# Half of the channel transform's outputs by plain float32 products, the rest by sums and differences

## The chip, the cores and the metric

The kernel runs on one core of a Trainium2 chip. The metric is the device time of one execution in microseconds (us). The core's engines are PE (matrix products; PEld is its weight load), DVE (VectorE), ACT (ScalarE), POOL (GpSimd) and SP, which here only issues DMAs. Each works through its own queue in order; they wait for each other through semaphores.

## The reference

The input is x of 2048 positions x 640 channels, float32. Two layers follow, each of a Fourier step and an attention step:

```python
def _A_ref(x, dft_seq_re, dft_seq_im, dft_hid_re, dft_hid_im):
    a = jnp.einsum("bsd,ed->bse", x, dft_hid_re)
    b = jnp.einsum("bsd,ed->bse", x, dft_hid_im)
    return jnp.einsum("ts,bse->bte", dft_seq_re, a) - jnp.einsum("ts,bse->bte", dft_seq_im, b)

def _B_ref(x, wqkv, wo):            # linear attention, 32 heads of 20
    q, k, v = ...                   # x @ wqkv
    phi = lambda t: jnp.where(t > 0, t + 1, jnp.exp(t)) + 1e-6
    kv = einsum(phi(k), v); z = sum(phi(k)); o = (phi(q) @ kv) / (phi(q) . z)
    return o @ wo

for _ in range(2):
    x = x + _A_ref(_layernorm(x), ...)
    x = x + _B_ref(_layernorm(x), B_wqkv, B_wo)
```

The matrices dft_hid_re and dft_hid_im are cosines and sines of 2 pi e d / 640. Cosine is even and sine odd under d -> 640 - d. Under e -> 320 - e both keep their size, and the sign depends on whether d is even or odd.

## The kernel before, in words

The 2048 positions are held as 16 tiles X[0] to X[15] of 128 x 640, in an order of positions and channels that puts mirror images side by side. The kernel trusts the symmetry of the four DFT matrices; `Check` compares all mirrored entries while the program runs, on DVE, and a slow general path stands behind a flag.

The Fourier step folds first: `script` walks a table of words (START for layer 0, SECOND for layer 1) and writes out, in that order, the sums and differences of mirrored channels (`f`, `d`), the layer norm, the sums and differences of mirrored positions, and the first part of the position transform (five sums of 512 columns, `u`). A word's last letter names the engine. Fetches of the channel matrices (`W`) and their split into a high and a low part (`w` on ACT, `v` on DVE) stand in the same tables. SECOND runs beside layer 0's attention outputs; each `|` is a pause until the next tile.

Then PLANS gives the order of the rest: `o1` is `outputs(1)`, the channel transform of one half of the positions; `s..` are the six other position sums (`whole`); `o0` is `outputs(0)`, the channel transform of the other half. In each `outputs` there are four groups r = 0 to 3. For each, `hidden` makes a real and an imaginary part in PSUM; ACT copies the imaginary part out, DVE forms difference and sum (`ym`, `yp`), and DVE and POOL add them to two tiles X (`lo` and `hi`), half a row at a time. `hidden` contracts over three blocks of 128 channels; each block takes three products of 322 columns in the split format (high x high, high x low, low x high), so nine a part. `keep` puts a position sum into SBUF as that high and low part: a copy on ACT and a subtraction on DVE.

The attention step follows at once. For each of the 16 tiles in turn (`keys_values`, tile positions n = 0 to 15) a tile is normalized, transposed on PE (L201) or through DMA, split, and multiplied with the key and the query weights (`product`, L250). Tile position n = 0 is X[8]; position 1 is X[11]. The layer norm's mean and variance come from DVE or ACT; the reciprocal root (`kept`, L163) and the shift (`nb`, L173) always come from POOL, in whose queue they stand behind the additions of `outputs`. `pksum`, the sum of the keys, is added up partly on POOL (L425).

Outside `script` a scheduler orders each engine's queue; it goes by a simulated timeline and the offsets of the AHEAD table, and the order is fixed when the program is built.

## Time and profile before

| | |
|---|---|
| median of 3 runs | 744.34 us (743.99 to 746.61) |
| span of the profiled execution | 742.7 us |
| PE busy | 722.4 us, 97% of the span |
| DVE, ACT, POOL busy | 599.4, 384.4, 262.9 us |
| granted PE clock | 0.997 over the span |
| DMA | 105.10 MB, mean 142 GB/s |

The span is the time from the first to the last instruction of one profiled execution; that execution's device time outside the profiler is not recorded, and the median of the runs lies 1.6 us above the span. In the rows of the timeline the first number is the start in us from the span's beginning, the second how long the engine was in it, then engine, line, operation, tiles and shapes, and the count; in brackets stands the idle time ahead and what ended it. PE's records overlap their successors, so a rate is read from start to start.

### The profile page before, as it was taken

Reading aid. Unit: us, or ns where it says so; the run is one execution under the profiler, and the core shown is the slowest. Engines: PE = TensorE matmul, PEld = TensorE weight load, DVE = VectorE, ACT = ScalarE, POOL = GpSimd, SP = SyncE. Lnnn points to the kernel's source line nnn. Section 1 sums busy time; section 2 is a strip of 40 time slices with the busy share of each in tenths; the row PEclk is TensorE's granted clock in tenths of the full one; section 3 lists DMA queues with packets and bytes.
Section 4 is the critical chain, followed back from the end, with each engine's and each line's share of the span. In section 5 each row is a group of like instructions: output and inputs, shape, how many; then the busy total and the mean of one; then the engine's idle time right before and its main releaser. Section 6 shows DMA issues by size and latency. Waiting matters only on the chain.

```text
span 742.7 us, 12890 instructions
## 1 busy us (share of the span) xinstructions
PE 722.4 (97%) x4762; PEld 691.3 (93%) x4762; DVE 599.4 (81%) x1147; ACT 384.4 (52%) x723; POOL 262.9 (35%) x293
## 2 busy tenths in 40 slices
PE   4899999999999999999999999999999999999997
PEld 1389999999999999899986999999999999999997
DVE  7999888878779785888887776967787888689983
ACT  7745654665445644445675337566632554443320
POOL 5237941331024311567772672136000010153220
PEclk9999999999999999999999999999999999999999
DMA  9333458562776836420001362645156663202553
GB/s 334 101 90 95 125 167 250 171 204 68 241 223 197 262 112 202 145 102 1 10 10 54 123 255 83 214 148 168 37 154 187 197 199 118 61 12 70 179 178 111
DMA packets 59005, 105.10 MB, mean 142 GB/s; under 512 B 5652, under 2 KB 23319, under 8 KB 58935
## 3 DMA queue, kind: packets, MB, share of 16 engines
q1 hardware_dynamic: 58935, 104.20, 44.2%
q8 instruction: 40, 0.66, 0.4%
q14 instruction: 30, 0.25, 0.1%
HBM read 78.99 MB, written 24.78 MB: 140 GB/s over the span
## 4 chain that ended last, share of the span: by engine, by line
PE 77%; DVE 11%; ACT 5%; DMA 2%; issue 1%; POOL 1%; SPq 1%; DVEq 0%; POOLq 0%; ACTq 0%
PE ps L250 49%; PE ps L355 16%; PE ps L1173 6%; PE ps L1099 4%; PE ps L201 2%; DVE w L189 1%; DVE t L189 1%; DMA raw<-in_wo 1%; DVE t L622 1%; DVE ps L615 1%; DVE ab L992 1%; DMA x<-in_x 1%; DVE x L644 1%; PE ps L543 1%; ACT ab L961 1%
## 5 line engine op out<-in xcount | busy, mean ns | idle before, releaser
L250 PE MATMUL ps<-w,t 128*128 128x320 f32 x2880 | 431.8, 310 | 0.5 <-DVE w L189 0.2
L250 PEld LDWEIGHTS ps<-w,t 128*128 128x128 f32 x2880 | 422.8, 188 | 1.4 <-DVE w L189 0.4
L355 PE MATMUL ps<-t,t 128*128 128x256 f32 (+1 forms) x640 | 139.8, 309 | 0.0
L1324 DVE CUSTOM_DVE_ANT_0 junk<-ck,ck 128x688 bf16<-128x688 f32 (+5 forms) x138 | 112.0, 812 | 8.2 <-DMA ck<-in_ck 6.6
L355 PEld LDWEIGHTS ps<-t,t 128*128 128x128 f32 x640 | 107.0, 188 | 0.0
L355 PE MATMUL ps<-w,t 128*128 128x384 f32 (+1 forms) x320 | 98.5, 310 | 0.6 <-DVE w L189 0.6
L388 ACT ACTIVATE t<-ps 128x640 f32<-128x640 f32 x64 | 45.1, 705 | 93.0 <-PE ps L250 89.3
L188 ACT CAST t<-t 128x640 fp32r<-128x640 f32 x62 | 45.1, 728 | 64.5 <-DVE t L218 29.3
L425 POOL TENSOR_TENSOR t<-t,s 128x640 f32<-128x640 f32 x17 | 30.5, 1792 | 118.0 <-DVE s L391 101.4
L599 POOL TENSOR_TENSOR t<-pq,t 128x640 f32<-128x640 f32 x25 | 40.0, 1610 | 74.6 <-ACT t L511 41.3
L355 PEld LDWEIGHTS ps<-w,t 128*128 128x128 f32 x320 | 60.1, 188 | 1.1 <-DVE w L189 0.9
L189 POOL TENSOR_TENSOR t<-t,t 128x640 fp32r<-128x640 f32 x14 | 22.8, 1631 | 92.8 <-ACT t L188 88.0
L189 DVE TENSOR_TENSOR t<-t,t 128x640 fp32r<-128x640 f32 x48 | 39.4, 820 | 15.6 <-ACT t L188 12.1
L391 DVE SCALAR_TENSOR_TENSOR pq<-t,pq 128x640 f32<-128x640 f32 x32 | 28.8, 899 | 23.8 <-ACT t L390 23.6
L390 ACT ACTIVATE t<-t 128x640 f32<-128x640 f32 x64 | 47.4, 741 | 0.0
L1173 PE MATMUL ps<-t,u 128*128 128x322 f32 x288 | 45.4, 314 | 0.4 <-DVE u L1156 0.4
L1173 PEld LDWEIGHTS ps<-t,u 128*128 128x128 f32 x288 | 43.2, 189 | 1.4 <-DVE u L1156 0.9
L188 ACT CAST t<-ps 128x640 fp32r<-128x640 f32 (+1 forms) x36 | 24.9, 691 | 35.5 <-PE ps L201 32.6
L391 DVE SCALAR_TENSOR_TENSOR s<-t,s 128x640 f32<-128x640 f32 x32 | 27.1, 847 | 15.8 <-ACT t L390 15.6
L1099 PE MATMUL ps<-cw,ab 128*128 128x512 f32 (+2 forms) x108 | 37.6, 500 | 2.0 <-ACT ab L962 1.2
L1099 PEld LDWEIGHTS ps<-cw,ab 128*128 128x128 f32 x108 | 19.9, 190 | 18.1 <-issue 12.9
L188 ACT CAST t<-s 128x640 fp32r<-128x640 f32 x32 | 23.3, 728 | 25.5 <-DVE t L189 18.6
(209 smaller groups left out, 1026.5 us busy)
## 6 DMA issues: line engine op xcount, KB each, us to landing
ck<-in_ck SPq DMA_DIRECT2D x48, 346.0 KB
ck<-in_ck SPq DMA_DIRECT2D x48, 344.0 KB
turn<-t SPq DMA_DIRECT2D x23, 320.0 KB
save<-w SPq DMA_DIRECT2D x20, 320.0 KB
w<-save SPq DMA_DIRECT2D x20, 320.0 KB
z<-turn SPq DMA_DIRECT2D x18, 320.0 KB
x<-in_x SPq DMA_DIRECT2D x16, 320.0 KB
out<-x SPq DMA_DIRECT2D x13, 320.0 KB
```

Source lines behind the costliest of these rows:

```text
L188: self.high = self.nc.scalar.copy(hi, src)
L189: return self.engine(pool).tensor_tensor(lo, src, hi.bitcast(F32), op=ALU.subtract)
L250: nc.tensor.matmul(pu[:m, 512 * h : 512 * h + HD], s, w[:, HD * h : HD * h + HD], start=first, stop=last)
L355: nc.tensor.matmul(self.place(G, c, part), x[:, 128 * c : 128 * c + 128], p[:, f : f + n], start=start and i == 0, stop=stop and i == 2, s ...
L388: nc.scalar.activation(h2(e), halves(pu), AF.Relu, scale=-1.0)
L390: nc.scalar.activation(e, e, AF.Exp, scale=-1.0)
L391: return k.ve.scalar_tensor_tensor(out, e, 1e-6, out, op0=ALU.add, op1=ALU.add)
L425: k.engine(n not in PKSUMS[k.layer]).tensor_tensor(pksum, pksum, pk, op=ALU.add)
L599: k.behind(k.nc.gpsimd.tensor_tensor(t1, self.PQ[self.order2[n]], self.zb, op=ALU.mult), lull)
L1099: self.k.nc.tensor.matmul(pu, s[:, cols : cols + 128], w[:, f : f + n], start=start and i == 0, stop=stop and i == len(todo) - 1)
L1173: self.k.nc.tensor.matmul(po[:, o : o + 322], s[:, f : f + 128], w[:, x, :], start=start, stop=stop)
L1324: i = nc.vector.tensor_tensor_reduce(k.junk[:, : a.shape[1]], b, a, 1.0, 0.0, op0, op1, o)
```

## The change

`hidden` now makes one plain float32 product for each of the three blocks, with 161, 322 and 161 columns, and with it only the outputs e = 0 to 160, for even and odd channels apart (the mirror e -> 320 - e then is a sum or a difference of the two). ACT and DVE form the real and imaginary parts' difference and sum as before, both into one tile `yy`; a new function `spread` adds the two parities for one set of outputs and subtracts them for the other, into `y`, with every second column written. One of its two instructions runs on DVE and one on POOL, in turns over the groups (SPREAD). The position sums are kept by one plain copy (`keep`), on ACT or DVE after KEPT and the tables, where there were a copy and a subtraction; the twelve memsets of `keep` on POOL go. The channel matrices are fetched whole (two DMAs of 128 x 644 a layer for six of 128 x 322) into work tiles, no longer through the `raw` buffers; their split goes, and one 2 x 161 scaling on ACT comes. The channels' order changes so that the two unmirrored channels stand first; the fold's slices and the layer norm's constants move with it. The check of the channel matrices compares eight or four mirror images in narrower pieces: 14 fetched tiles for 12, and one more checking step, at tile position 14 of layer 1.

The core of the diff:

```diff
-CKH = 344
-CKHN = 3
+CKH = (102, 135)
+CKHN = (2, 3)
+QN = 161
+HW = (0, 161, 483, 644)
+HP = (((0, 161), (0, 322), (161, 161)), ((161, 161), (0, 322), (0, 161)))
+SPREAD = ("vp", "pv")
-START = '... x11d f7v ... x01d k9a ... kda w02a fcv fdv w00a nfa w01a nea a3v b3v v00v c3v v01v t3v V1a v02v t1v t2v t0v w11a u23v w10a u21v u20v u24v v11v u22v w12a v12v v10v g0a ...'
+START = '... x11d W1d f7v ... x01d W0d w0a k9a ... kda fcv fdv nfa nea a3v b3v c3v t3v V1a t1v t2v t0v u23v u21v u20a u24a u22a g0a ...'
-SECOND = '... x11d W00d W01d W02d W10d | w00a | w01a v00W W11d | w02a v01v W12d | v02v | R0a V0a w10a | O0p sfa v10v ... | w11a c2v v11v H20v w12a nfa nea v12v ... u20v u21v u23v u24v u22v'
+SECOND = '... x11d W1d W0d w0a | | | | | R0a V0a | O0p sfa ... | c2v H20v nfa nea ... u20a u21v u23v u24a u22a'
+KEPT = ("ava", "vav")
...
-        steps = STEPS[0], STEPS[1] if ...
+        steps = STEPS[0] + (14,) * self.k.layer, STEPS[1] if ...
...
-    def hidden_fetch(self, par, c):
-        raw = self.k.raw.tile([128, 322], F32, tag="raw", name=self.k.nm("rawh"))
-        self.k.nc.sync.dma_start(raw, self.hid[par][c])
-    def hidden_high(self, par, c, raw): ...
-    def hidden_low(self, par, c, raw, eng): ...
+    def hidden_fetch(self, par):
+        t = self.k.temp(shape=(128, HW[3]))
+        self.k.nc.sync.dma_start(t, self.hid[par])
+        self.hw[par] = t
+    def hidden_scale(self):
+        self.k.nc.scalar.mul(self.hw[0][0:2, :QN], self.hw[0][0:2, :QN], 0.5)
...
     def keep(self, ci, c, pu, e=None):
-        hi, lo = (pool.tile([128, 640], F32R, tag=tag, name=k.nm("u")) for _ in range(2))
+        u = k.wp.tile([128, 640], F32, tag="w", name=k.nm("u"))
+        copy = nc.scalar.copy if e == "a" else nc.vector.tensor_copy
-            nc.scalar.copy(hi[:, :512], pu)
-            eng.tensor_tensor(lo[:, :512], pu, hi[:, :512].bitcast(F32), op=ALU.subtract)
+                copy(u[:, :512], pu)
...
     def hidden(self, ci, f, po, o):
-        order = (1, 2, 0) if ci == 3 else range(3)
+        order = (1, 2, 0) if ci == 3 else (1, 0, 2)
         for i, c in enumerate(order):
-            for s, x, start, stop in ((hi, 0, i == 0, False), (hi, 1, False, False), (lo, 0, False, i == 2)):
-                self.k.nc.tensor.matmul(po[:, o : o + 322], s[:, f : f + 128], w[:, x, :], start=start, stop=stop)
+            u, (at, n) = self.UT[min(ci, 2), c + 2 if ci == 3 else c], HP[ci % 2][c]
+            self.k.nc.tensor.matmul(
+                po[:, o + at : o + at + n], u[:, f : f + 128], self.hw[ci % 2][:, HW[c] : HW[c + 1]],
+                start=i == 0, stop=i == 2, skip_group_check=True,
+            )
+
+    def spread(self, y, x, by):
+        e = {"v": self.k.ve, "p": self.k.nc.gpsimd}
+        pairs = lambda t: t.rearrange("p g (b i) -> p g b i", b=2)
+        e[by[0]].tensor_tensor(y[:, :, 0 : 2 * QN - 1 : 2], x[:, :, :QN], x[:, :, QN:], op=ALU.add)
+        e[by[1]].tensor_tensor(
+            y[:, :, : 2 * QN - 2].rearrange("p g (b i two) -> p g b i two", b=2, two=2)[:, :, :, :, 1],
+            pairs(x[:, :, : QN + 1])[:, :, :, : QN // 2], pairs(x[:, :, QN - 1 :])[:, :, :, 1:], op=ALU.subtract,
+        )
...
-                nc.vector.tensor_tensor(ym, p[:, :322], yi, op=ALU.subtract)
-                nc.vector.tensor_tensor(yp, p[:, :322], yi, op=ALU.add)
+                nc.vector.tensor_tensor(yy[:, 0, :], p[:, :322], yi, op=ALU.subtract)
+                nc.vector.tensor_tensor(yy[:, 1, :], p[:, :322], yi, op=ALU.add)
+                self.spread(y, yy, SPREAD[r % 2])
```

How it moves the queues is shown at two places. In the changed program the lines of `product`, the transposes, the statistics and the key sum are L253, L204, L161/L166/L176 and L428 for L250, L201, L158/L163/L173 and L425; `hidden` is L1152 for L1173, and `spread` is L1161 (sums) and L1162 (differences).

The first place is layer 0, where `outputs(0)` begins and tile position 0 of the attention is transposed in its midst. POOL's queue before, from the last group of `outputs(1)` (L1216, L1205) to the reciprocal root of X[8] (kept_718):

```order
L1216 TENSOR_TENSOR x_130<-x_130,t_610 128x321
L1205 TENSOR_TENSOR x_124<-x_124,t_610 128x319
L1159 MEMSET u_642 128x31
L1159 MEMSET u_642 128x95
L158 TENSOR_SCALAR ve_719<-kept_718 128x1
L158 TENSOR_SCALAR ve_907<-kept_906 128x1
L1159 MEMSET u_656 128x31
L1159 MEMSET u_656 128x95
L158 TENSOR_SCALAR ve_1007<-kept_1006 128x1
L1159 MEMSET u_670 128x31
L1159 MEMSET u_670 128x95
L163 TENSOR_TENSOR kept_718<-ve_719,mhalf 128x1
```

and now (the root of X[8] is kept_620):

```order
L1161 TENSOR_TENSOR t_531<-t_530 128x322
L1210 TENSOR_TENSOR x_116<-x_116,t_512 128x321
L1211 TENSOR_TENSOR x_116<-x_116,t_512 128x319
L1198 TENSOR_TENSOR x_114<-x_114,t_512 128x319
L161 TENSOR_SCALAR ve_621<-kept_620 128x1
L161 TENSOR_SCALAR ve_766<-kept_765 128x1
L1210 TENSOR_TENSOR x_128<-x_128,t_531 128x321
L1211 TENSOR_TENSOR x_128<-x_128,t_531 128x319
L1198 TENSOR_TENSOR x_122<-x_122,t_531 128x319
L161 TENSOR_SCALAR ve_866<-kept_865 128x1
L166 TENSOR_TENSOR kept_620<-ve_621,mhalf 128x1
```

A `spread` instruction has joined each group, and the memsets are gone; the root still stands behind all four groups. PE's queue before (t_717 is X[8] normalized; t_386, t_392 and t_380 hold one channel matrix):

```order
L1173 MATMUL ps_767<-t_386,u_656 128x322 x2
L1173 MATMUL ps_767<-t_386,u_657 128x322
L1173 MATMUL ps_767<-t_392,u_670 128x322 x2
L1173 MATMUL ps_767<-t_392,u_671 128x322
L1173 MATMUL ps_767<-t_380,u_642 128x322 x2
L1173 MATMUL ps_767<-t_380,u_643 128x322
L201 MATMUL ps_786<-ident,t_717 128x128 x5
L1173 MATMUL ps_757<-t_426,u_683 128x322 x2
L1173 MATMUL ps_767<-t_426,u_683 128x322 x2
```

and now (t_619 is X[8] normalized; t_341 and t_238 hold the two channel matrices):

```order
L1152 MATMUL ps_659<-t_238,u_546 128x322
L1152 MATMUL ps_663<-t_238,u_546 128x322
L1152 MATMUL ps_659<-t_238,u_587 128x161
L1152 MATMUL ps_659<-t_238,u_553 128x161
L1152 MATMUL ps_663<-t_238,u_587 128x161
L1152 MATMUL ps_663<-t_238,u_553 128x161
L204 MATMUL ps_670<-ident,t_619 128x128 x5
L1203 MATMUL ps_690<-t_341,u_579 1x322
L1203 MATMUL ps_690<-t_341,u_570 1x161
```

The five transposes now follow both parts of two groups, where they followed the real parts alone.

The second place is layer 1, where `outputs(0)` ends and the attention begins. POOL's queue before, from the additions of the last groups to the key sum (kept_5087 and nb_5093 are the root and the shift of X[11], tile position 1; s_5085 are the keys of position 0):

```order
L1205 TENSOR_TENSOR x_100<-x_100,t_4998 128x319
L373 MEMSET t_5075 128x640
L1217 TENSOR_TENSOR x_110<-x_110,t_5026 128x319
L1205 TENSOR_TENSOR x_108<-x_108,t_5027 128x319
L162 TENSOR_SCALAR ve_5088<-kept_5087 128x1
L158 TENSOR_SCALAR ve_5183<-kept_5182 128x1
L163 TENSOR_TENSOR kept_5087<-ve_5088,mhalf 128x1
L163 TENSOR_TENSOR kept_5182<-ve_5183,mhalf 128x1
L173 TENSOR_TENSOR nb_5093<-kept_5087 128x1
L173 TENSOR_TENSOR nb_5190<-kept_5182 128x1
L175 TENSOR_SCALAR nb_5190<-nb_5190 128x1
L425 TENSOR_TENSOR t_5075<-t_5075,s_5085 128x640
```

and now (kept_4807, nb_4813 and s_4805):

```order
L1161 TENSOR_TENSOR t_4745<-t_4744 128x322
L376 MEMSET t_4795 128x640
L1211 TENSOR_TENSOR x_100<-x_100,t_4726 128x319
L1198 TENSOR_TENSOR x_98<-x_98,t_4726 128x319
L1198 TENSOR_TENSOR x_106<-x_106,t_4745 128x319
L165 TENSOR_SCALAR ve_4808<-kept_4807 128x1
L161 TENSOR_SCALAR ve_4903<-kept_4902 128x1
L1211 TENSOR_TENSOR x_108<-x_108,t_4745 128x319
L166 TENSOR_TENSOR kept_4807<-ve_4808,mhalf 128x1
L166 TENSOR_TENSOR kept_4902<-ve_4903,mhalf 128x1
L428 TENSOR_TENSOR t_4795<-t_4795,s_4805 128x640
L176 TENSOR_TENSOR nb_4813<-kept_4807 128x1
```

A `spread` instruction stands ahead of the last additions (one more a row before these), and the key sum has moved from behind the shift nb to ahead of it. PE's queue before, in the query product of tile position 0 (t_5086 is X[11] normalized; t_4923 and t_4924 are the split X[8]; t_5153 is the split X[11]):

```order
L250 MATMUL ps_5134<-w_5063,t_4924 128x320 x2
L250 MATMUL ps_5134<-w_5067,t_4923 128x320 x2
L201 MATMUL ps_5147<-ident,t_5086 128x128 x5
L250 MATMUL ps_5134<-w_5068,t_4923 128x320 x2
L250 MATMUL ps_5134<-w_5067,t_4924 128x320 x2
L250 MATMUL ps_5134<-w_5071,t_4923 128x320 x2
L250 MATMUL ps_5204<-w_5035,t_5153 128x320 x2
L250 MATMUL ps_5204<-w_5036,t_5153 128x320 x2
```

and now (t_4806 is X[11] normalized; t_4674, t_4675 and t_4873 are the split tiles):

```order
L253 MATMUL ps_4854<-w_4787,t_4675 128x320 x2
L253 MATMUL ps_4854<-w_4791,t_4674 128x320 x2
L253 MATMUL ps_4854<-w_4792,t_4674 128x320 x2
L253 MATMUL ps_4854<-w_4791,t_4675 128x320 x2
L204 MATMUL ps_4867<-ident,t_4806 128x128 x5
L253 MATMUL ps_4924<-w_4755,t_4873 128x320 x2
L253 MATMUL ps_4924<-w_4756,t_4873 128x320 x2
L253 MATMUL ps_4924<-w_4755,t_4874 128x320 x2
```

The transposes have moved from the midst of the query product to its end, and the next key product, which needs their split result, follows directly.

More of the change, by code (lines that the diff above doesn't have):

```diff
@@ L119, in __init__ @@
         nc.gpsimd.memset(self.tiny, 1e-6)
-        self.two = self.cst.tile([128, 2], F32, name="two")
-        nc.vector.tensor_scalar(self.two, self.ident[:, 0 : 65 : 64], -1.0, 2.0, op0=ALU.mult, op1=ALU.add)
     def nm(self, s):
@@ L803, in script @@
         order = [(w[0], int(w[1], 16), w[2:-1], w[-1]) for w in order.replace("|", "|0-").split()]
-        raw = {}
         summed = {i for kind, i, c, e in order if kind == "s" and e == "q"}
@@ L884, in script @@
             elif kind == "W":
-                raw[g, int(c)] = four.hidden_fetch(g, int(c))
+                four.hidden_fetch(i)
             elif kind == "x":
@@ L888, in script @@
             elif kind == "w":
[L889 to L893 removed]
+                four.hidden_scale()
             elif kind == "H":
@@ L899, in script @@
             elif kind == "u":
-                four.keep(2, int(c), four.sum(int(c)), eng)
+                four.keep(2, int(c), four.sum(int(c)), e)
             else:
@@ L1410, in fast_path @@
     pieces.sort(key=lambda p: p[0])
-    pieces += [(2 + m, 2 * m, ckh[m][f]) for m in range(2) for f in range(CKHN)]
+    pieces += [(2 + m, 4 if m or f > 1 else 0, ckh[m][f]) for m in range(2) for f in range(4 - m)]
     order = [0, 3, 4, 7, 1, 2, 5, 6]
```

134 lines of the change are left out of this document (65 added, 69 removed).

## The prediction, as it was written before the result was known

> **What bounds the kernel now.** I read the page first (busy shares and groups), then PE's timeline through the four stages that the change touches, then the queues of POOL, DVE and ACT at the places where PE goes on from a Fourier step into the attention.
>
> ```profile
> span 742.7 us, 12890 instructions
> PE 722.4 (97%) x4762; PEld 691.3 (93%) x4762; DVE 599.4 (81%) x1147; ACT 384.4 (52%) x723; POOL 262.9 (35%) x293
> L1173 PE MATMUL ps<-t,u 128*128 128x322 f32 x288 | 45.4, 314 | 0.4 <-DVE u L1156 0.4
> ```
>
> PE is busy 97% of the span; what shortens PE's own queue shortens the kernel, as long as no other engine's work then comes late. The channel products (L1173) are 288 records and 45.4 us, with 0.4 us of waiting. The stages on PE in layer 0 and in layer 1:
>
> ```profile
> 33.23 8.87 PE L1099 MATMUL ps<-cw,ab 128*128 128x512 f32 x20 [0.22 <-ACT ab L961]
> 41.65 11.38 PE L1173 MATMUL ps<-t,u 128*128 128x322 f32 x72
> 52.86 4.92 PE L1099 MATMUL ps<-cw,ab 128*128 128x256 f32 x22
> 57.43 0.47 PE L1137 MATMUL ps<-cx,ex 128*128 128x258 f32 x1
> ...
> 63.42 3.05 PE L1173 MATMUL ps<-t,u 128*128 128x322 f32 x18
> 66.31 0.71 PE L201 MATMUL ps<-ident,t 128*128 128x128 f32 x5
> 66.77 1.88 PE L1173 MATMUL ps<-t,u 128*128 128x322 f32 x11
> ...
> 75.83 6.29 PE L250 MATMUL ps<-w,t 128*128 128x320 f32 x42
> ```
>
> ```profile
> 404.71 10.99 PE L1173 MATMUL ps<-t,u 128*128 128x322 f32 x72 [0.44 <-DVE u L1156]
> 415.54 5.55 PE L1099 MATMUL ps<-cw,high 128*128 128x256 f32 x45
> ...
> 422.93 0.90 PE L1173 MATMUL ps<-t,u 128*128 128x322 f32 x5
> 423.67 0.71 PE L201 MATMUL ps<-ident,t 128*128 128x128 f32 x5
> ...
> 435.13 7.49 PE L250 MATMUL ps<-w,t 128*128 128x320 f32 x50
> 442.47 0.71 PE L201 MATMUL ps<-ident,t 128*128 128x128 f32 x5
> ```
>
> The reader sees PE going from stage to stage with almost no bracket: outputs(1) takes 11.21 us in layer 0 (41.65 to 52.86) and 10.83 in layer 1; outputs(0), with five transposes and one extra row, 12.41 and 12.20. But beside these stages POOL and DVE are nearly full:
>
> ```profile
> 53.00:64.00 11.00, 11.00 (x55) 9.71 (x54) 10.72 (x28) 4.25 (x10) 10.91 (x21) 1.00 0.00 1
> 76.00:100.00 24.00, 24.00 (x169) 23.98 (x169) 20.70 (x40) 14.68 (x25) 23.36 (x30) 1.00 0.40 117
> 417.00:435.00 18.00, 18.00 (x135) 17.99 (x134) 13.73 (x28) 5.66 (x12) 11.18 (x17) 1.00 0.82 299
> ```
>
> Columns: stage, length, then busy time of PE, PEld, DVE, ACT, POOL. POOL works 10.91 of 11 us and 23.36 of 24 in layer 0, on the additions that `outputs` leaves behind. PE has no idle time there, POOL has none to give.
>
> **The change on PE.** Before, a part (real or imaginary, of one group) is nine products: 72 in 11.21 us, 155.7 ns each, 1.40 us a part. After, it is three plain products of 161, 322 and 161 columns. A plain product leaves two records: layer 0's 20 position products of 512 columns stand in the trace as 40, the last 20 of them from 33.23 to 41.65, 421 ns each; the 22 of 256 columns from 52.86 to 57.43 take 208 each. That is 0.82 ns a column and record with almost nothing fixed. So 322 columns cost 265 ns, and 161 cost 132 in proportion; the upper end is the 155.7 of a split record with 322 column passes. I take 138, nearer the proportion, since neither plain row shows a fixed part. A part is then 4 x 138 + 2 x 265 = 1.08 us (1.06 to 1.15). A stage of eight parts is 8.65 us. outputs(1) gains 2.56 and 2.18; outputs(0), with a ninth product for the row (1.08) and 0.47 for the transposes, becomes 10.2 and gains 2.2 and 2.0. Together 8.95 us (7 to 9.6).
>
> The Trainium skill ("FP8 and Floating Point Precision", TensorE Precision Notes) speaks against so much: true FP32 takes four passes through the array. Priced as four times a split record's column (155.7 / 322 = 0.484 ns), a part would cost 644 x 4 x 0.484 = 1.25 us and the four stages would gain only about 5 us; the rows above put a plain column at 1.64 ns, not 1.93, and I follow them.
>
> **Smaller gains.** The position sums' copy replaces copy and subtraction, and the split of the matrices goes:
>
> ```profile
> L189 DVE TENSOR_TENSOR u<-ps,u 128x512 fp32r<-128x512 f32 x12 | 8.1, 676 | 0.9 <-ACT u L188 0.8
> L1156 DVE TENSOR_TENSOR u<-ps,u 128x512 fp32r<-128x512 f32 x10 | 6.6, 684 | 0.3
> L1111 ACT ACTIVATE t<-rawh 128x322 fp32r<-128x322 f32 x8 | 3.8, 469 | 0.0
> L1324 DVE CUSTOM_DVE_ANT_0 junk<-ck,ck 128x688 bf16<-128x688 f32 x42 | 39.9, 949 | 2.2 <-DMA ck<-in_ck 1.8
> ```
>
> PE's wait of 0.44 us at 404.71 was for that subtraction, and the 0.22 at 33.23 stands behind ACT's work in START, from which three L1111 of 0.47 go and one scaling of 2 rows comes. I count 0.65 us (0 to 1). The rest is off the path: half of the 22 subtractions become copies on ACT, DVE's matrix splits go, and the checks shrink from 6 pieces of 1,720 compared columns to 4 of 918 and 3 of 1,215. PE covers all of it. The extra check step at position 14 of layer 1 is two pieces, some 3.5 us of DVE by the L1324 row, in a stage where DVE waits for PE; without that cover it would cost this much once. The fetches move the same bytes or fewer, in the same queue ahead of the weights, and leave the raw buffers free earlier; the weights' splits are limited later by POOL and cost or gain nothing. Shifted fold slices keep their widths.
>
> **What the spread costs.** Sixteen pairs come: one instruction of a pair on DVE, one on POOL, of 322 elements each with two SBUF inputs. The nearest rows are the additions beside them:
>
> ```profile
> L1216 POOL TENSOR_TENSOR x<-x,t 128x321 f32<-128x321 f32 x13 | 13.0, 1000 | 0.0
> L1204 DVE TENSOR_TENSOR x<-x,t 128x321 f32<-128x321 f32 x16 | 14.3, 898 | 0.0
> L1201 DVE TENSOR_TENSOR t<-ps,t 128x322 f32<-128x322 f32 x16 | 7.8, 484 | 4.3 <-ACT t L1198 3.1 <-ACT t L1200 0.9
> ```
>
> So 1.0 us on POOL (about 0.95 from start to start) and 0.5 to 0.9 on DVE. Writing every second column is free on DVE: the L189 row writes so, at 676 ns against 684 for the dense L1156. POOL shows no such write; I take it as free there too. POOL's price is 3.8 us a stage, less the memsets. It matters where POOL's queue ends in a value that PE waits for.
>
> *Layer 0, transposes of X[8].*
>
> ```profile
> 49.93 1.57 POOL L880 TENSOR_TENSOR ab<-ab,ab 128x640 f32<-128x640 f32 x1 [21.86 <-DVE ab L878]
> 51.45 1.13 POOL L1217 TENSOR_TENSOR x<-x,t 128x319 f32<-128x319 f32 x1
> ...
> 61.53 0.86 POOL L1205 TENSOR_TENSOR x<-x,t 128x319 f32<-128x319 f32 x1
> ...
> 63.58 1.63 POOL L163 TENSOR_TENSOR kept<-ve,mhalf 128x1 f32<-128x1 f32 x3
> 64.19 0.61 DVE L182 TENSOR_SCALAR t<-x,kept 128x640 f32<-128x640 f32 x1 [0.48 <-POOL kept L163]
> ```
>
> Twelve additions run from 51.45 to 62.39, 0.91 each; the root follows at 63.58 and DVE's norm ends at 64.80, 1.5 us before PE transposes at 66.31. Now the first spread goes ahead of L880, which I put 0.8 us earlier since DVE has lost three splits; then 15 instructions of 0.91 end at 64.3, and variance, root and norm (1.8) at 66.1. PE comes earlier: 41.4 + 8.65 + the six position sums (63.42 - 52.86 = 10.56) + four parts (4.3) = 64.9. A wait of 1.2 us (0 to 3). The next tiles have POOL work of layer 0's outputs(0) ahead of them as before; by the same count the tile at position 3 arrives just in time.
>
> *Layer 1, start of outputs(0).* The first product needs the fifth position sum's copy, which DVE now has to fit in behind four spread halves: 0.5 us (0 to 1).
>
> *Layer 1, tile position 1.* This is the large term.
>
> ```profile
> 438.05 1.13 POOL L1205 TENSOR_TENSOR x<-x,t 128x319 f32<-128x319 f32 x1
> 439.26 0.31 POOL L162 TENSOR_SCALAR ve<-kept 128x1 f32<-128x1 f32 x1
> ...
> 439.83 1.09 POOL L163 TENSOR_TENSOR kept<-ve,mhalf 128x1 f32<-128x1 f32 x2
> 440.89 0.34 POOL L173 TENSOR_TENSOR nb<-kept 128x1 f32<-128x1 f32 x2
> ...
> 443.61 1.56 POOL L425 TENSOR_TENSOR t<-t,s 128x640 f32<-128x640 f32 x1 [2.05 <-DVE s L391]
> 441.12 0.92 ACT L176 ACTIVATE t<-x,nb,kept 128x640 f32<-128x640 f32 x1
> ```
>
> With T the first key product (435.13): the last addition ends at T+4.0, the root begins at T+4.7, the shift at T+5.8, ACT's norm ends at T+6.9 and PE transposes at T+7.3: 0.4 us to spare. Now POOL begins again 5 us after the stage's start (PE 3.5, ACT 0.5, DVE 0.9) and has 9 additions, 4 spreads, a row and a memset (13 x 0.95 + 1.1) ahead of the root: it is done 19.5 us after the stage's start, which is T+9.1 as T comes 10.3 after it. Behind the root stands the key sum, 1.56 us, then the shift, then the norm on ACT (0.92): T+12.0. PE has finished position 0's 60 products at T+8.8 (50 take 7.34) and waits 3.2 us; as the next product directly follows the transposes, ACT's cast of their result (0.7 and the way there) no longer hides: 1.2 more. Together 4.4 us; 1 if POOL runs at its shortest intervals (0.84) and a spread is cheap, 6 at 1.1 each. Nothing returns it: PE is the bound for the next 180 us.
>
> **Sum.** -8.95 - 0.65 + 1.2 + 0.5 + 4.4 = -3.5 us. Against the span, 742.7 to 739.2; the median of the runs is 1.6 us above the span, and I carry the difference over: 744.34 - 3.5 = 740.8 us. A measurement of this kernel can tell about 0.5% from no change, that is 3.7 us: 740.6 and below is faster, 748.1 and above slower. The forecast lies at the edge.
>
> **Rivals.**
> - *The waits hide (0.25).* DVE and POOL get back on time since 11 subtractions, 12 splits and 12 memsets are gone; POOL's shift then arrives before T+8.8. For it: POOL has 11.18 of 18 us in 417 to 435. Against: the key sum is queued ahead of the shift. Left are 9.6 less 1.5: 736.2 us.
> - *DVE and POOL exclude each other (0.12).* An L1204 addition takes 898 ns where the L1201 with a PSUM input takes 484: beside POOL, DVE's work from SBUF doubles. If the spread halves always block each other, a group of outputs(0) in layer 1 needs 4 x 0.87 on POOL and 3 x 0.48 on DVE, 4.9 us against PE's 2.2; the root comes 1 us later still, and position 3 of layer 0 2 us late: 743.8 us. The Trainium skill ("SBUF — State Buffer", the section on the two sides and the shared pair) calls that pair an exclusive lock held for the whole instruction; the doubled rows agree.
> - *The plain product is dearer (0.06).* At 1.25 us a part the gain is 5.7 and PE comes later, so that waits shrink to 4: 742.6 us. The 421 ns rows speak against it.
> - *Slower (0.10).* POOL's strided write costs more than a dense one. Each 0.1 us on a POOL half is on the way to four transposes in layer 0, four more by position 3, and four to eight at layer 1's position 1: some 14 halves, 1.4 us. From 1.45 us a half, by half above the row, the kernel is slower by over 0.5%; at 1.6, what 640 elements cost here (the 1.56 of L425), it is 750 us.
>
> **How the numbers follow.** My case has 0.47 and a range of its own of 738.5 to 743.5, so 0.22 of it is faster by over 0.5% and 0.25 within. Faster: 0.22 + 0.25 = 0.47. Within: 0.25 + 0.12 + 0.06 = 0.43. Slower: 0.10. The range of 735.5 to 745.5 leaves out the slower rival and the ends.
>
> **What the new profile would show.** L1152 records of 322 columns 265 ns apart, of 161 about 138, and outputs(1) in 8.6 to 8.8 us: right on PE. In layer 1 a bracket of 3 us or more before L204 or the following L253, put down to ACT, with POOL's L428 ahead of L176: right on the wait. A PE without such brackets is the first rival; L1161 and L1162 on POOL above 1.4 us the last. I would be wrong altogether if PE's stages shrank and a later stage gave it back, as the checks or the output weights' fetches.

## The result, and the profile after

The changed kernel takes 755.59 us (754.66 to 755.87), the kernel before 745.34 beside it: a ratio of 1.014 (95% interval 1.0122 to 1.0158). It is slower by 1.4%; the forecast was 740.8, and its range ended at 745.5. With each group of experiments the kernel before ran again, at 744.45 to 745.61, and each ratio below is against the runs beside it. Two runs, 1448.86 us of the kernel before and 889.95 us of an experiment, were slow ones and are left out of the ratios.

The span went from 742.7 to 753.7 us. PE is busy for 720.5 us in the kernel after, 1.9 less than before, and the span is 11 us longer, so PE waits more. PE's timeline after, first in layer 0, then in layer 1:

```profile
41.70 8.88 PE L1152 MATMUL ps<-t,u 128*128 128x322 f32 x48
50.42 5.26 PE L1097 MATMUL ps<-cw,ab 128*128 128x256 f32 x22
...
59.34 2.32 PE L1097 MATMUL ps<-cw,ab 128*128 128x256 f32 x10
64.42 4.60 PE L1152 MATMUL ps<-t,u 128*128 128x322 f32 x24 [2.76 <-DVE u L1141]
...
71.83 4.62 PE L1152 MATMUL ps<-t,u 128*128 128x322 f32 x24 [1.09 <-DVE t L192]
76.18 6.41 PE L253 MATMUL ps<-w,t 128*128 128x320 f32 x42
...
87.76 4.10 PE L253 MATMUL ps<-w,t 128*128 128x320 f32 x26 [1.40 <-DVE t L192]
91.70 0.71 PE L204 MATMUL ps<-ident,t 128*128 128x128 f32 x5
```

```profile
405.54 8.89 PE L1152 MATMUL ps<-t,u 128*128 128x322 f32 x48
414.15 5.65 PE L1097 MATMUL ps<-cw,high 128*128 128x256 f32 x45
...
423.69 1.05 PE L1152 MATMUL ps<-t,u 128*128 128x322 f32 x4 [1.88 <-DVE u L1141]
...
436.17 9.07 PE L253 MATMUL ps<-w,t 128*128 128x320 f32 x60
450.28 1.33 PE L204 MATMUL ps<-ident,t 128*128 128x128 f32 x5 [5.04 <-ACT t L179]
452.39 6.14 PE L253 MATMUL ps<-w,t 128*128 128x320 f32 x30 [0.78 <-ACT t L191]
458.36 0.71 PE L204 MATMUL ps<-ident,t 128*128 128x128 f32 x5
```

outputs(1) is as short as forecast: 8.72 us (41.70 to 50.42) and 8.61. What follows has brackets that the timeline before did not have. The longest stands where the forecast put it, ahead of the transposes of layer 1's tile position 1. From the first key product to the transposes of position 2 it was 13.93 us before (435.13 to 449.06); it is 22.19 now (436.17 to 458.36). Three rows of the kernel before: first the transposes of position 2 in layer 0, then the end of that stretch in layer 1.

```profile
89.55 0.71 PE L201 MATMUL ps<-ident,t 128*128 128x128 f32 x5
...
442.93 6.29 PE L250 MATMUL ps<-w,t 128*128 128x320 f32 x40
449.06 0.71 PE L201 MATMUL ps<-ident,t 128*128 128x128 f32 x5
```

The waits do not make all of it: the five transposes of position 1 now take 1.33 us instead of 0.71, and 30 products 6.14 where 40 took 6.29 before. In the windows of the kernel after (columns as before: busy time of PE, PEld, DVE, ACT, POOL, and then PE's granted clock, 1.00 for full speed) the clock around these two places is halved for 3.41 us (from 424.9) and for 6.83 us (from 448.8), so the windows are laid at steps of 3.41:

```profile
421.48:424.89 3.41, 1.53 (x10) 1.19 (x10) 2.92 (x7) 0.67 (x2) 3.41 (x5) 1.00 0.98 300
424.89:428.30 3.41, 3.41 (x11) 1.61 (x10) 0.82 (x1) 0.69 (x1) 0.89 (x2) 0.50 1.02 394
...
445.35:448.76 3.41, 0.00 (x0) 0.00 (x0) 0.43 (x1) 0.00 (x0) 3.41 (x5) 1.00 0.00 0
448.76:452.17 3.41, 1.33 (x5) 0.93 (x5) 0.00 (x0) 1.45 (x2) 0.90 (x4) 0.50 0.00 0
452.17:455.58 3.41, 3.19 (x12) 3.19 (x13) 3.21 (x10) 3.41 (x8) 0.00 (x0) 0.50 0.01 2
```

Behind each stretch in which PE was busy for less than half (1.53, 0.00 and 1.33 of 3.41 us) stands one at clock 0.50. So a wait can be paid a second time: behind the 1.88 us before outputs(0) of layer 1, PE runs at half speed for 3.41 us. It isn't always: the 2.76 us in layer 0 fell across two such stretches, with PE busy for 1.98 and 2.08 of 3.41 us (59.67 to 63.08 and 63.08 to 66.50); a clock of 1.00 followed, and the 24 products there took 4.60 us.

Four rows of DVE show what the first product of outputs(0) waited for, the copy of a sum (L1136) and of its one further column (L1141), first in layer 0, then in layer 1. PE ended the last sum at 61.66 and 421.80; DVE came to these copies at 63.60 and 422.86, behind other work in its queue.

```profile
63.60 0.67 DVE L1136 COPY u<-ps 128x512 f32<-128x512 f32 x1
64.19 0.15 DVE L1141 COPY u<-ps 128x1 f32<-128x1 f32 x1
...
422.86 0.68 DVE L1136 COPY u<-ps 128x512 f32<-128x512 f32 x1
423.46 0.14 DVE L1141 COPY u<-ps 128x1 f32<-128x1 f32 x1
```

And the queues of POOL and ACT in layer 1, up to the long wait:

```profile
430.85 1.06 POOL L1162 TENSOR_TENSOR t<-t 128x320 f32<-128x320 f32 x1 [5.07 <-DVE t L1194]
...
446.53 1.09 POOL L166 TENSOR_TENSOR kept<-ve,mhalf 128x1 f32<-128x1 f32 x2
447.59 1.53 POOL L428 TENSOR_TENSOR t<-t,s 128x640 f32<-128x640 f32 x1
449.08 0.34 POOL L176 TENSOR_TENSOR nb<-kept 128x1 f32<-128x1 f32 x2
449.31 0.92 ACT L179 ACTIVATE t<-x,nb,kept 128x640 f32<-128x640 f32 x1 [6.51 <-POOL nb L176]
```

From 430.85 POOL works with two short gaps (0.49 and 0.26 us, both for DVE); root, key sum, shift and norm follow in the forecast's order. The root is done at 447.62, 11.4 us behind the first key product, where the forecast had it done at 9.1.

### The profile page after: what moved, and what is told of

It reads as the page before. It is cut to its first block, busy times and chain, and to the rows that moved or that the text cites. A ratio compares the mean times of both kernels' runs of the same rounds, so it can differ in the third digit from the quotient of the medians.

```text
span 753.7 us, 12667 instructions
## 1 busy us (share of the span) xinstructions
PE 720.5 (96%) x4666; PEld 679.7 (90%) x4666; DVE 590.8 (78%) x1139; ACT 374.2 (50%) x701; POOL 277.1 (37%) x299
## 4 chain that ended last, share of the span: by engine, by line
PE 67%; DVE 17%; ACT 7%; POOL 3%; issue 3%; DMA 2%; SPq 1%; DVEq 0%; POOLq 0%; ACTq 0%
PE ps L253 45%; PE ps L358 15%; PE ps L1097 2%; DVE w L192 2%; DVE t L192 1%; PE ps L204 1%; PE ps L1152 1%; ACT t L922 1%; ACT t L923 1%; ACT ab L959 1%; DVE x L647 1%; DVE t L625 1%; DMA raw<-in_wo 1%; DVE x L1197 1%; DVE ps L618 1%
## 5 line engine op out<-in xcount | busy, mean ns | idle before, releaser
L253 PE MATMUL ps<-w,t 128*128 128x320 f32 x2880 | 433.3, 310 | 2.5 <-DVE t L192 1.4
L253 PEld LDWEIGHTS ps<-w,t 128*128 128x128 f32 x2880 | 424.0, 188 | 3.8 <-DVE t L192 1.8
L1318 DVE CUSTOM_DVE_ANT_0 junk<-ck,ck 128x692 bf16<-128x692 f32 (+7 forms) x141 | 110.0, 780 | 9.6 <-DMA ck<-in_ck 8.4
L428 POOL TENSOR_TENSOR t<-t,s 128x640 f32<-128x640 f32 x17 | 30.7, 1804 | 112.3 <-DVE s L394 112.3
L192 POOL TENSOR_TENSOR t<-t,t 128x640 fp32r<-128x640 f32 x14 | 23.7, 1692 | 100.0 <-ACT t L191 95.2
L192 DVE TENSOR_TENSOR t<-t,t 128x640 fp32r<-128x640 f32 x48 | 39.5, 824 | 16.0 <-ACT t L191 11.5
L192 DVE TENSOR_TENSOR t<-ps,t 128x640 fp32r<-128x640 f32 (+1 forms) x36 | 29.3, 813 | 19.6 <-ACT t L191 18.7
L1152 PE MATMUL ps<-t,u 128*128 128x161 f32 (+1 forms) x192 | 37.0, 350 | 5.7 <-DVE u L1141 4.6
L1152 PEld LDWEIGHTS ps<-t,u 128*128 128x128 f32 x192 | 30.4, 192 | 13.2 <-issue 6.4
```

The source lines that it names most:

```text
L192: return self.engine(pool).tensor_tensor(lo, src, hi.bitcast(F32), op=ALU.subtract)
L253: nc.tensor.matmul(pu[:m, 512 * h : 512 * h + HD], s, w[:, HD * h : HD * h + HD], start=first, stop=last)
L428: k.engine(n not in PKSUMS[k.layer]).tensor_tensor(pksum, pksum, pk, op=ALU.add)
L1152: self.k.nc.tensor.matmul(po[:, o + at : o + at + n], u[:, f : f + 128], self.hw[ci % 2][:, HW[c] : HW[c + 1]], start=i == 0, stop=i == 2, ...
L1318: i = nc.vector.tensor_tensor_reduce(k.junk[:, : a.shape[1]], b, a, 1.0, 0.0, op0, op1, o)
```

## The experiments

Each kernel is the changed one with the edit shown. In most of them theory A says that queue order at POOL and DVE makes the waits; theory C, formed when both halves on DVE had cost time, says that DVE and POOL hold each other up. The half clock has a theory A of its own in the two experiments on it.

**Copies on ACT.**

```diff
-KEPT = ("ava", "vav")
+KEPT = ("aaa", "aaa")
```

> All six copies of the position sums go to ACT (in the changed kernel three of six stand in DVE's queue). Theory A (the changed kernel waits at the start of outputs(0), 2.76 us in layer 0 and 1.88 in layer 1, because the first product now reads the middle sum, whose copy DVE reaches late): PE's waits put down to L1141 fall from 4.6 us to about 1.7, PE's clock stays at 1.0 behind the one in layer 1, and the time falls by 3 to 5 us, from 755.6 to 751 or 752; the wait of 5 us before the transposes of layer 1's tile position 1 stays. Rival (those waits only move what POOL would make late anyway): the wait shifts to the transposes or to the next product, and the time stays at 754 to 756.

Measured: 750.19 us (ratio 1.0072, 1.0047 to 1.0096), by the ratios 5 us less than the changed kernel. The waits for L1141 are gone from PE's list, and the half clock in outputs(0) of layer 1 with them (1.00 from 421 to 425). Others came: 1.46 us for X[8]'s norm, behind POOL's root, and 1.89 at layer 0's position 1, where ACT's norm came after DVE's L1194; the 5.08 us in layer 1 stayed. Theory A holds for this wait, the rival for part of it.

**Statistics of layer 1's position 1 on DVE.**

```diff
-ASTATS = ((4, 10, 11, 13, 14), (1, 4, 8, 10))
+ASTATS = ((4, 10, 11, 13, 14), (4, 8, 10))
```

> Only the statistics of tile position 1 of layer 1 (X[11], complete since outputs(1)) move from ACT to DVE; POOL's root and shift for it then stand ahead of outputs(0)'s additions and spread halves, with all of those halves still there. Theory A (PE's 5.04 us wait and the half clock after it come from the root's and the shift's place in POOL's queue): the wait before those transposes goes, the granted clock stays at 1.0 there, and the time falls by 7 to 8.5 us, to about 747.5. Rival (DVE and POOL are too slow with the spread in any order, and the next tile then waits instead): the time falls by under 3 us, to 752.5 or more.

Measured: 749.11 us (1.0061, 1.0038 to 1.0084). POOL's row and PE's rows of this kernel:

```profile
427.81 0.19 POOL L176 TENSOR_TENSOR nb<-kept 128x1 f32<-128x1 f32 x1
...
436.09 6.43 PE L253 MATMUL ps<-w,t 128*128 128x320 f32 x42
...
450.28 0.71 PE L204 MATMUL ps<-ident,t 128*128 128x128 f32 x5
```

The shift is there 21 us earlier, the wait has gone, and the stretch to position 2 is 14.19 us instead of 22.19. The long wait was the place in POOL's queue, as the forecast said. The time fell by less than those 8 us: in the profiled run the 2.76 us wait of layer 0 now was followed by a half clock (24 products in 6.28 us, not 4.60).

**Both edits.** 

> Both edits: all copies of the sums on ACT, and the statistics of layer 1's tile position 1 on DVE. If the two waits are independent, their gains add: 755.6 - 4 - 8 = about 743.5, the same as the kernel before or a little faster. If the PE gain of the plain products (8.95 us by the forecast, about 6.5 as the stages of the changed kernel stand) is to be kept, other waits must not grow: 740 would mean that the forecast's sum holds without these two; 747 or more that a third place (layer 0's first tiles) has taken it back.

Measured: 746.28 us (1.0022, 1.0006 to 1.0038), with single runs from 744.91 to 750.09. The gains add in part: the expected 743.5 was missed by 2.8 us. The profiled run, the slowest of the ten (750.09), shows further places that take time, waits of 1.5 and 2.1 us in layer 0 and of 1.8 and 1.7 in layer 1.

**No spread.**

```diff
-                self.spread(y, yy, SPREAD[r % 2])
+                y = yy
```

> The changed kernel without the spread's sixteen pairs: the additions take the two halves as ACT and DVE left them, so that the channel transform's other outputs are wrong in this kernel (the row keeps its own spread). Theory A (the spread's load on POOL and DVE makes the layer 1 wait): POOL reaches the root about 5 to 6 us earlier, the wait of 5 us and the half clock go, the wait at the start of outputs(0) shrinks too, and the time falls to 742 to 746. Rival B (queue order alone: roots and sum copies stand behind the additions in any case): the time falls by 3 us or less, to 752 or more.

Measured: 739.90 us (0.9938, 0.9914 to 0.9961). The spread costs 15.7 us (755.6 - 739.9); the forecast had given it 6.1 (1.2 + 0.5 + 4.4). All that the change gains without it is 5 us. PE's rows of layer 1, undisturbed:

```profile
417.81 1.08 PE L1152 MATMUL ps<-t,u 128*128 128x322 f32 x4
418.73 0.71 PE L204 MATMUL ps<-ident,t 128*128 128x128 f32 x5
419.37 0.97 PE L1203 MATMUL ps<-t,u 128*1 128x322 f32 x4
420.27 1.63 PE L1152 MATMUL ps<-t,u 128*128 128x161 f32 x8
421.83 0.43 PE L1203 MATMUL ps<-t,u 128*1 128x161 f32 x2
422.20 6.80 PE L1152 MATMUL ps<-t,u 128*128 128x322 f32 x36
428.73 7.61 PE L253 MATMUL ps<-w,t 128*128 128x320 f32 x50
```

outputs(0) takes 10.92 us here (417.81 to 428.73), against 12.20 before. In this pair of profiled runs the spans differ by 15.4 us (753.7 and 738.3), of which some 3.7 are half clock: 1.56 in outputs(0) of layer 1 (12.48 and 10.92), 0.62 in the transposes of position 1 and 1.5 in the 30 products behind them.

**A filled wait.** Products whose result nothing reads, into free columns of the transposes' PSUM tile, layer 1, ahead of position 1 (the main lines of the edit):

```diff
+                    if n == 0 and k.layer:
+                        for i in range(28):
+                            nc.tensor.matmul(tp[:, 640:960], x[0][i % 5], W[1][i % 5][0][:, :320], start=True, stop=True, skip_group_check=True)
```

> Work is added: 28 products of 320 columns (0.148 us each by the rows of the attention, 4.1 us) whose result nothing reads, in both layers' program only for layer 1, ahead of the transposes of tile position 1 where PE waits 5.04 us. Theory A (the clock is granted by how busy PE was in a stretch of some 3.4 us, so the wait costs a second time, as 6.5 us at half clock behind it): the granted clock stays at 1.0 from 449 to 456, the transposes still begin when POOL's shift allows, but take 0.71 us instead of 1.33 and the 30 products behind them 4.6 instead of 6.1; the kernel gets faster by 1.5 to 2.5 us, to about 753.5, although PE does more. Rival (the half clock has another cause, such as the plain float32 products before it): the half clock stays and the time is 755 or more; the work that was added cannot make it faster.

Measured: 753.47 us (1.0121, 1.0100 to 1.0142). The time is as its theory A has it, but the profile does not decide: 0.96 us of waiting was left ahead of the transposes and 0.78 behind, and the clock there was 0.76 and 0.74 in windows of 4 and 3 us. With 32 products ahead and 5 behind:

> The changed kernel with 32 idle products of 0.148 us ahead of the transposes of layer 1's tile position 1 and 5 behind them, so that PE is busy through the whole wait (a first try with 28 left 0.96 and 0.78 us of idle time within one stretch, and the clock was halved behind them all the same). Theory A (a stretch of 3.4 us in which PE is busy less than about half halves the clock in the next): the granted clock is 1.0 from 440 to 460, the 30 products behind take 4.6 us instead of 6.1, and the time is 752.5 to 754 against 755.6, with 5.5 us more work on PE. Rival (the half clock comes from something else): the clock is 0.5 there again and the time is 755.5 or more.

Measured: 753.42 us (1.0125, 1.0097 to 1.0153). Windows, then PE rows, of this kernel:

```profile
448.00:452.00 4.00, 3.00 (x18) 2.47 (x19) 1.52 (x6) 2.41 (x5) 0.00 (x0) 1.00 0.01 2
452.00:456.00 4.00, 4.00 (x31) 3.99 (x30) 3.21 (x9) 3.12 (x7) 1.23 (x3) 1.00 0.00 0
```

```profile
448.22 0.77 PE L425 MATMUL ps<-ident,t 128*128 128x128 f32 x5 [0.39 <-ACT t L180]
...
450.50 4.95 PE L254 MATMUL ps<-w,t 128*128 128x320 f32 x30 [0.78 <-ACT t L192]
```

With PE kept busy, the same place runs at clock 1.00: the transposes take 0.77 us, the 30 products 4.95. The half clock there came from PE's idle time. The intervals of the ratios overlap with the changed kernel's (1.0122 to 1.0158), so a gain of 2 us is likely, not shown; the rows are what decides.

**Both halves on DVE; both on POOL.**

```diff
-SPREAD = ("vp", "pv")
+SPREAD = ("vv", "vv")      # the other kernel: ("pp", "pp")
```

> Both halves of each spread on DVE, none on POOL. Theory A (POOL's queue makes the layer 1 wait; a DVE half takes 0.48 us where POOL isn't working and 0.97 beside it): POOL comes 4 us earlier to the shift, the wait of 5 us goes below 2, and so does the half clock behind it; DVE's copies of the sums come about as late as before; the time falls by 5 to 8 us, to 748 to 750. Rival (DVE and POOL share one path to SBUF, so that it doesn't matter on which of them a half runs): the waits stay and the time is within 2 us of 755.6.

> Both halves of each spread on POOL. By theory A POOL needs 4 us more in each of the four stages, which in layer 1 goes straight into the wait for tile position 1 (5 becomes 8 or 9 us) and in layer 0 into the waits for the first two tiles: 762 to 768. By the rival (one shared path) DVE's other work gets faster by as much and the time rises by less than 3 us, to at most 758.

Measured: 761.89 us (1.0223, 1.0186 to 1.0259) and, in a single run, 759.64. The first expectation missed by its sign: POOL rid of 16 instructions makes the kernel 6 us slower. The second (762 to 768) and both rivals missed too. Neither engine has room for the halves, and that DVE hasn't is what the forecast overlooked.

**A DVE half with one input in PSUM.** ACT copies one of the two inputs back into the products' PSUM tile first; both halves on DVE.

```diff
+                z = p.rearrange("p (a b) -> p a b", a=2)[:, :, :322]
+                nc.scalar.copy(z[:, :, :QN], yy[:, :, :QN])
-                self.spread(y, yy, SPREAD[r % 2])
+                self.spread(y, yy, SPREAD[r % 2], z)      # first input from z
```

> Against the run with both halves on DVE (761.9 us): there each half reads two SBUF inputs; here ACT first copies the first of the two halves of its input back into the PSUM tile that the products left, so that each DVE half reads one input from PSUM. Same 32 halves in DVE's queue, POOL's queue unchanged, 16 copies of 0.4 us more on ACT. Theory C (an instruction of DVE with two SBUF inputs and one of POOL exclude each other, so that DVE and POOL together, not POOL alone, are what PE waits for): the halves take 0.48 us also beside POOL, POOL's additions get back to 0.75 to 0.85, and the time falls to 744 to 750. Rival (DVE simply has too many instructions in its queue): the halves stay in it, with one more hop through ACT, and the time stays at 758 or more.

Measured: 752.47 us (1.0091, 1.0068 to 1.0114), 9.4 us less than with both inputs in SBUF, although ACT has 16 copies more. The groups of the two kernels, first with SBUF inputs, then with one in PSUM:

```profile
L1161 DVE TENSOR_TENSOR t<-t 128x322 f32<-128x322 f32 x16 | 12.1, 756 | 0.1
L1162 DVE TENSOR_TENSOR t<-t 128x320 f32<-128x320 f32 x16 | 11.6, 725 | 0.0
L1198 POOL TENSOR_TENSOR x<-x,t 128x319 f32<-128x319 f32 x16 | 18.3, 1141 | 21.8 <-DVE t L1162 21.8
```

```profile
L1162 DVE TENSOR_TENSOR t<-ps,t 128x322 f32<-128x322 f32 x16 | 7.7, 481 | 2.5 <-ACT ps L1197 2.5
L1163 DVE TENSOR_TENSOR t<-ps,t 128x320 f32<-128x320 f32 x16 | 7.7, 478 | 0.0
L1201 POOL TENSOR_TENSOR x<-x,t 128x319 f32<-128x319 f32 x16 | 16.1, 1009 | 18.9 <-DVE t L1163 18.9
```

The same sums on the same engine go from a mean of 0.74 us to 0.48, and POOL's additions beside them from 1.14 to 1.01 (the two other groups of POOL additions gain less, 1.01 to 0.95 and 0.88 to 0.84). A PSUM input is not faster in itself: with SBUF inputs the shortest half took 0.47 us, the median 0.48 to 0.50, and the longest 1.8, so the mean comes from halves that were held up. DVE's own additions from SBUF got slower (L1197, now L1200: 0.70 to 0.91). All this is as theory C has it, and its rival, 758 or more, fell. The expected 744 to 750 was missed by 2.5 us. The Trainium skill ("SBUF — State Buffer", the section on its two separate sides) says that a DVE instruction with two SBUF inputs and a GpSimd one that reads SBUF take a shared port pair in turns, each for its whole length; the runs agree.

**The halves one by one.** Only POOL's, then only DVE's, their results not read:

> The changed kernel with only those halves of the spread that run on POOL (one a group); their result is not read, and the additions take DVE's sums as in the run without any spread (739.9 us), so that part of the channel transform's outputs is wrong in this kernel. Theory of the prediction (the POOL halves make the waits): most of the 15.7 us between 739.9 and 755.6 comes back, to 750 or more. Theory C (the two engines hold each other up): both halves cost alike, 743 to 749.

> The counterpart: only those halves that run on DVE, not read either. Theory of the prediction: DVE has time beside PE, so next to nothing comes back, 740 to 742. Theory C: each of these halves stops POOL for half a microsecond and waits for it as long, 743 to 749; the two runs' increases over 739.9 together are well under 15.7 us if the waits start only when both loads are there.

Measured: 749.02 us (1.0046, 1.0027 to 1.0066) and 749.98 (1.0067, 1.0043 to 1.0091). Over the 739.9 without any, POOL's 16 halves cost 9.1 us and DVE's 10.1 (by the ratios 8.0 and 9.6), about as much each. The first run decides nothing, as it lies between the two theories; the second does, since the forecast had DVE's halves at nothing (740 to 742). Theory C's 743 to 749 was passed by up to 1 us, and its guess that both together stay well under 15.7 missed: they come to 19.2. PE's waits tell where each kind is paid, first with POOL's halves alone, then with DVE's (in all, times, longest):

```profile
PE ps L204 <- ACT t L179: 4.8, 1, 4.8
...
PE ps L1152 <- DVE u L1141: 2.5, 1, 2.5
PE ps L1097 <- DVE t L1196: 2.4, 1, 2.4
PE ps L204 <- ACT t L179: 1.8, 1, 1.8
```

POOL's halves alone bring back the long wait at layer 1's position 1, with a half clock behind it (30 products in 6.55 us), and no wait for the sums' copies. DVE's halves alone bring back the waits for the copies (2.49 us in layer 1, 1.58 for L1136 in layer 0) and one for DVE's L1196 in layer 0 (2.42 us); 1.79 us are left at position 1. So each engine's queue ends in a value of its own that PE waits for, and DVE's does so as well as POOL's.

**Repairs together.** PSUM input for both halves on DVE and copies on ACT, then with the statistics on DVE too:

> The same with all copies of the sums on ACT. Theory C: the waits at the start of outputs(0) go as they did before (3 to 5 us), and the time falls to 740 to 744, at or below the kernel before (744.5). Rival: ACT now has the copies and the halves' copies in one queue and is late for both; 748 or more.

> Spread on DVE with one PSUM input, copies of the sums on ACT (747.7 us so far), and the statistics of layer 1's tile position 1 on DVE, so that its root and shift stand ahead of outputs(0)'s additions on POOL. If POOL's queue is what is left of the layer 1 wait (2.8 us, with a half clock in some runs), it goes and the time is 743 to 745, level with the kernel before. If DVE is late instead, the wait moves to the next tile and the time stays at 746.5 or more.

Measured: 747.70 us (1.0033, 1.0016 to 1.0050) and 744.80 (0.9995, 0.9977 to 1.0012). The second is level with the kernel before, as expected; in its profiled run PE still waits 2.7 us in outputs(0) of layer 0 and 1.5 at layer 1's position 2. The expectation for the first was missed by 3.7 us: ACT's copy of the row, behind weight casts that waited for their DMA, came 2.70 us late for PE in layer 0, with a half clock behind it (12 products in 4.13 us, 2.45 in the second kernel), and 2.77 us of waiting stayed at layer 1's position 1.

One more run sets the second beside its like without the PSUM input: both halves on DVE from SBUF, copies on ACT, statistics on DVE. It was expected at 741 to 744 us, or at 746 and more if DVE was what came late. It took 750.43 us (1.0073, 1.0048 to 1.0098), with waits of 4.1 and 2.1 us for ACT's and DVE's casts in layer 0. The PSUM input alone is the difference to 744.80: 5.6 us, and the intervals of the two ratios do not touch. Two more variants of the second (row and its spread on DVE) were run:

> The same, with the row's copy and spread on DVE (its copy on ACT stood behind weight casts and held up PE by 2.7 us in layer 0) and the extra checking step at tile position 13 instead of 14 (at 14 the key sum that DVE owes PE comes 0.66 us late). If both waits are gone without another: 2 to 3 us less than the run before this one, 740.5 to 742.5, at or under the kernel before. If something else ends the same time (the spread's load on DVE in layer 0), no difference: within 1 us of it.

> As the second of these runs but with the extra checking step at position 14 again, and the real parts of outputs(0) start with the two products of 161 columns, whose sums are copied first, instead of the middle one of 322 columns, whose sum comes last. If the start of outputs(0) still waits, this gives PE 0.5 us of work there and the time is 0.3 to 1 us under what the step alone would leave; with all copies on ACT that wait may be gone already, and then the time equals the second run plus the 0.66 us of the checking step: 741 to 743.

Measured: 747.28 us (1.0025, 1.0005 to 1.0045) with the checking step at position 13, and 744.89 (1.0002, 0.9984 to 1.0020) with it at 14 and the other order; the latter loses part of outputs(0)'s real sums, so that its time tells of the queue alone. Neither hit: with the step at position 13 PE's wait at L503 is gone and another is there (0.9 us for ACT's step L392 of the keys), and the row on DVE is late like it was on ACT (3.4 and 2.7 us). Which of the two edits makes the first of these kernels slower than the second repair is not separated. No version that forms all outputs beat the kernel before.

## Why the prediction was wrong, point by point

The stages of PE, from start to start in the two profiled runs, against the terms of the forecast (us; the key products begin at 75.83 and 435.13 before, at 76.18 and 436.17 after):

| stage | forecast | measured |
|---|---|---|
| up to outputs(1), both layers (smaller gains) | -0.65 | -1.81 |
| outputs(1), both layers | -4.74 | -4.71 |
| layer 0, position sums and start of outputs(0) | 0 | +3.44 |
| layer 0, outputs(0) with X[8] | -1.0 | -0.65 |
| layer 0, first key product to the transposes of position 2 | 0 | +1.80 |
| layer 1, position sums and start of outputs(0) | +0.5 | +2.15 |
| layer 1, outputs(0) | -2.0 | +0.28 |
| layer 1, first key product to the transposes of position 2 | +4.4 | +8.26 |
| the rest | 0 | +2.24 |
| span | -3.5 | +11.0 |

- *The gain on PE.* Right for outputs(1): 2.49 and 2.22 us (forecast 2.56 and 2.18), and a part is 8.61 / 8 = 1.08 us, as worked out. With it falls the rival by which a plain product is dearer, 1.25 us a part. outputs(0) gained 1.3 in layer 1 without the spread (12.20 to 10.92), not 2.0: its row takes 1.27 us (0.90 and 0.37), not 1.08, the transposes 0.64, not 0.47, and the eight parts 9.01, not 8.65.
- *The wait at layer 1's position 1.* Right in place, order and releaser, too small in size: 4.4 us forecast, 8.26 measured. POOL came 2.3 us later than counted, and some 2.1 us are half clock (0.62 in the transposes, 1.5 in the products, with 4.6 for 30 at full clock), which the forecast did not have. Its count of POOL left out the two variances ahead of the root (1.0 us) and the two gaps for DVE (0.75).
- *The start of outputs(0).* Mis-sized: 0.5 us in layer 1 was 1.88 and a half clock (outputs(0) 12.48 us, where the run without spread has 10.92); in layer 0, forecast at nothing here, it was 2.76. The first product now reads the middle sum, which PE makes among the last, and its copy was DVE's.
- *The transposes of X[8]* did not wait for the norm as forecast (1.2 us), since PE came late itself; with the copies on ACT that wait is there (1.46 us), so the term was hidden, not wrong. Two other waits stand in the stage and behind it (1.09 and 1.40 us, both for DVE's L192).
- *The step that failed* is the costing of the spread: "It matters where POOL's queue ends in a value that PE waits for." DVE's half was taken as work beside other work. The runs showed that each half costs some 0.6 us of time on either engine (9.1 and 10.1 us for 16): PE waits for values from DVE's queue too, the copies of the sums first of all, and DVE and POOL, both busy for 14.00 of the 14 us before outputs(0) of layer 0 (50 to 64), lengthen each other's work. How the 10.1 us divide between the place in DVE's queue and this lengthening is not shown; the PSUM input, which takes away the second (and adds copies on ACT), was worth 5.6 us for 32 halves. The forecast's own rival saw it from the doubled L1204 row, but priced it at 3 us more and gave it 0.12; the rival "slower" had the sign with another mechanism, which fell: with both on POOL the halves took 0.86 and 0.95 us in the mean, no more than the dense additions beside them (0.85 to 0.93).
- *Smaller gains* came, and larger: 1.86 us in layer 1 ahead of outputs(1) (PE's wait of 0.44 us for L1156 is gone, among others). The cover named for the extra checking step was not there: DVE's key sum came late by 0.66 us at PE's L503.

Open is how much of the spread's cost is half clock in other runs than the two profiled ones: it depends on where a wait falls, and runs of one kernel differ in it.

## What to carry to other kernels

Where a change moves work from a full PE to engines beside it, follow the queue of each of these engines, not of one alone, to the values that PE waits for, and compare it with the stage, not with the engine's share of the span. Where DVE and POOL both read two inputs from SBUF, count a DVE instruction at what it takes beside POOL (here 0.73 to 1.1 us in the mean for 322 columns, 0.48 alone). Find out which copy the first product of a new order needs, and whether a small value stands behind bulk work in a queue. Reckon that a PE wait that fills half of a stretch of some 3.4 us can cost nearly its own length again (1.88 us of waiting brought 1.56 us of slower work here, 5.82 us brought 2.1), or nothing.

## What was not expected of the hardware

The clock's grain. Where the clock was halved in these profiles, it was for stretches of 3.41 us, or for several such in a row, and what went before decided it only in part. The wait of 2.76 us in layer 0 fell across two stretches in the kernel after, each more than half busy, and the 24 products behind it ran at full clock in 4.60 us. In the run with the statistics on DVE it lay inside one, in which PE was busy for 0.65 us, and they took 6.28:

```profile
62.43:65.84 3.41, 0.65 (x3) 0.47 (x3) 3.41 (x11) 0.00 (x0) 3.41 (x8) 1.00 0.00 0
65.84:69.26 3.42, 3.42 (x12) 2.86 (x12) 3.42 (x6) 0.00 (x0) 3.42 (x5) 0.50 0.47 141
```

So it matters whether a wait falls into one stretch or across two. Shorter waits lie at an edge. The 1.88 us before outputs(0) of layer 1 left PE busy for 1.53 of 3.41 us in the kernel after, and the clock was 0.50 behind it; in the filled kernel the wait there was 1.87 us, again inside one stretch:

```profile
421.25:424.66 3.41, 1.54 (x10) 1.23 (x9) 2.63 (x6) 0.67 (x2) 3.41 (x5) 1.00 0.90 339
424.66:428.08 3.42, 3.42 (x18) 2.03 (x17) 1.12 (x2) 1.45 (x3) 0.61 (x1) 1.00 1.02 374
```

Behind that one the clock stayed at 1.00. What decides at this edge is not shown. The Trainium skill ("TensorE: Matmul & The Clock Gate", Part 1) gives a free-running window of 3.4 us and advises against idle gaps longer than that; here a gap of little more than half of it was enough.
